# Moving DMA transposes, output stores and three pairs of state copies to other places and queues in a fused linear-attention and SwiGLU kernel

## The chip, the cores and the metric

The kernel runs on 1 core of one Trainium2 chip. The metric is device time in microseconds (us); profiled spans are about 2 us shorter than the timed runs of the same kernel. Engines: PE (TensorE), DVE (VectorE), ACT (ScalarE), POOL (GpSimd) and SP (SyncE, which here only issues DMAs). "Clock" is the share of its full clock that PE was granted.

## The reference, cut to what matters

Batches of 768 tokens go through causal linear attention with a decaying state; the result x goes through a SwiGLU layer.

```python
for b in range(nb):                       # blocks of the sequence, state carried along
    intra = einsum(qb, kb) * Dmask;  intra = einsum(intra, vb)
    inter = einsum(qb * lam_pow, kv_state)
    out[:, :, sl] = intra + inter
    kv_state = lam_block * kv_state + einsum(kb * rev_pow, vb)
# x: 3072 x 512
g = x @ w_gate;  silu = g / (1 + exp(-g))
return (silu * (x @ w_val)) @ w_out
```

Inputs and output are float32; the kernel multiplies in bfloat16. The reference's blocks have 64 tokens, the kernel's 128.

## The kernel before

The kernel works on 24 blocks of 128 tokens (4 batches of 6). A block needs three loads, issued on POOL (k and q are cast to bfloat16 on the way), then k and q transposed, `scores` (k times q), `cluster` (the output of attention and the new state), and its share of the feed-forward layer. Blocks 0 to 7 are transposed on PE, blocks 8 to 23 by DMA from the sync queue. The order of the program is the order of every engine and queue.

```python
    def load_kq(n):                                   # k and q of block n, cast to bf16
        t = ld.tile([128, 2, H, D], BF16, name="kq_nat", tag="kq")
        nc.gpsimd.dma_start(out=t[:, 0], in_=k5[b, j])
        nc.gpsimd.dma_start(out=t[:, 1], in_=q5[b, j])
    def load(n):
        load_kq(n)
        load_v(n, nc.gpsimd)                          # v stays float32
    # ... cut ...
    def transposes(n):
        t = apool.tile([128, 2, HP, BLK], BF16, name="qkT", tag="qkT", bufs=6)
        if n >= PE_T:                                 # PE_T = 8
            nc.sync.dma_start_transpose(out=t..., in_=state.pop(("kq", n))...)
        # ... else: on PE ...
    # ... cut: inside cluster(n, scores_of) ...
        if scores_of is not None:
            scores(scores_of)                         # needs transposes(scores_of)
        # ... x = xT on VectorE, matmuls "up", kv_st = kv_dec + up on VectorE ...
            bd = kv_bd[(n + 1) % 2]                   # the next block's inter matmuls need it
            for h2 in range(2):
                if n < PE_T:
                    nc.scalar.copy(out=bd[...], in_=st[r])
                else:
                    nc.gpsimd.tensor_copy(out=bd[...], in_=st[r])
    # ... cut: end of ffn_out ...
        nc.scalar.copy(out=osb, in_=op)
        nc.sync.dma_start(out=out[t0:t0 + 128, :], in_=osb)
    # ... cut: the schedule of the third tile of tokens ...
    for per in range(4):
        for pos in range(3):
            ffn_fc(2, 3 * per + pos)
            if pos == 2:
                ffn_out(*outs.pop(0))                 # one output store each
            if (per, pos) == (0, 2):
                scores(8)
                transposes(10)
            elif (per, pos) == (1, 0):
                cluster(8, 9)
                scale_v(10)
                load(12)
            elif (per, pos) == (1, 2):
                cluster(9, 10)
                transposes(11)
                scale_v(11)
                load(13)
            elif (per, pos) == (2, 1):
                cluster(10, 11)                       # needs transposes(11)
                # ... transposes(12), scale_v(12), load(14), and so on
```

## Time and profile before

| | before |
|---|---|
| median before the prediction (3 runs) | 247.18 us |
| profiled span, mean clock | 245.9 us, 0.976 |
| PE busy | 228.5 us, 93% |

The windows view gives the busy time of each engine in a stretch (number of instructions in brackets), then the clock, the share of the DMA engines and what they moved. Kernel before:

```profile
core 0: us, PE busy (x) PEld busy (x) DVE busy (x) ACT busy (x) POOL busy (x), PEclk, DMA share, GB/s
62.00:72.50 10.50, 10.28 (x111) 6.58 (x110) 5.10 (x9) 2.35 (x6) 3.35 (x6) 1.00 0.66 100
72.50:82.00 9.50, 2.54 (x32) 1.89 (x26) 2.50 (x5) 0.77 (x2) 6.78 (x9) 0.74 1.73 129
82.00:88.90 6.90, 6.68 (x46) 3.84 (x44) 2.57 (x4) 0.48 (x2) 4.06 (x6) 0.62 0.62 96
95.00:200.00 105.00, 104.37 (x722) 51.31 (x733) 47.50 (x69) 28.53 (x48) 44.21 (x62) 1.00 0.67 100
```

Nearly everywhere PE has no time to win: 104.37 of 105 us from 95 to 200. From 72.5 to 82 us it works 2.54 of 9.5 us. From 82 to 88.9 it is busy all the time, but with 46 instructions at a clock of 0.62: busy is not fast.

The chain that ended last, in order of time (start, length, what), around that hole:

```profile
62.31 2.32 PE yp L299 x10
69.05 2.54 PE yp L299 x11
...
72.76 9.01 DMA qkT<-kq_nat
81.78 0.05 issue
81.82 0.61 PE sp L207 x6
...
85.25 3.51 PE yp L299 x11
...
92.44 2.54 PE yp L299 x11
...
242.23 0.59 ACT osb L302
```

PE waits for a DMA transpose, and afterwards eleven matmuls that take 2.54 us elsewhere take 3.51. The timeline has PE's own waits, in brackets at the end of a line:

```profile
75.37 0.40 PE L221 MATMUL op<-qkT,kv_bd 128*128 128x128 bf16 x4 [0.91 <-POOL kv_bd L253]
81.82 0.61 PE L207 MATMUL sp<-qkT 64*128 64x128 bf16 x8 [6.05 <-DMA qkT<-kq_nat]
```

What stood on the sync queue (L303 is an output store, L184 a transpose):

```profile
65.28 0.36 SPq L303 DMA_DIRECT2D out_dram<-osb  x1
65.82 1.30 SPq L184 DMA_TRANSPOSE qkT<-kq_nat  x1
72.24 0.35 SPq L303 DMA_DIRECT2D out_dram<-osb  x1
72.76 9.09 SPq L184 DMA_TRANSPOSE qkT<-kq_nat  x2
```

The transpose at 72.76 us is that of block 11. The view of one line's instructions, for that transpose alone, gives its time to landing:

```profile
L184 SPq DMA_TRANSPOSE qkT<-kq_nat x1: 1488/1488/1488, 72.8 to 72.8; - x1
DMA to landing us min/median/max: 9.0/9.0/9.0
```

For the one at 65.82 us the same view says 3.1. So the transpose was issued late, behind a store, and then landed slowly.

### The profile page before, as it was taken

The page shows a single profiled execution, that of the slowest core. Times are in us where ns is not written, and L with a number is a line of the kernel's source. Part 1 is how long each engine was busy: PE and PEld are TensorE (multiplying, and loading weights), DVE is VectorE, ACT ScalarE, POOL GpSimd, SP SyncE. Part 2 cuts the span into 40 slices and gives each one's busy share as a digit, 9 for nine tenths or more (in the row PEclk, how much of TensorE's full clock was granted, in tenths as well). Part 3 has the DMA queues.
Part 4 walks back from the last instruction along what each step waited for, and adds up shares of the span by engine and source line. Part 5 has one row for each costly group of instructions (what it writes and reads, how often), then busy time and mean ns, then how long its engine had stood idle before and what let it go on. Part 6 is the DMA issues. An engine that isn't in the chain of part 4 may idle for free.

```text
span 245.9 us, 4376 instructions
## 1 busy us (share of the span) xinstructions
PE 228.5 (93%) x1730; PEld 125.0 (51%) x1754; DVE 104.8 (43%) x171; ACT 80.6 (33%) x158; POOL 114.9 (47%) x155
## 2 busy tenths in 40 slices
PE   7879999999991699999999999999999999999993
PEld 3456745788660464555455444455445444444441
DVE  1855636586552432562463354355256222322200
ACT  6556634646220023122212213313222222332121
POOL 8897979929078191447636750844331000000000
PEclk9999999999997599999999999999999999999998
DMA  6999999999929989998599595289301110111022
GB/s 131 195 190 211 188 218 163 188 207 147 162 33 155 136 107 172 108 128 117 99 146 119 94 204 126 52 120 131 87 0 45 43 41 2 45 43 43 19 109 85
DMA packets 83171, 28.32 MB, mean 115 GB/s; under 512 B 71056, under 2 KB 78736, under 8 KB 83152
## 3 DMA queue, kind: packets, MB, share of 16 engines
q0 software_dynamic: 57456, 16.26, 61.5%
q1 hardware_dynamic: 25696, 11.80, 21.8%
q8 instruction: 13, 0.21, 0.4%
q14 instruction: 6, 0.05, 0.1%
HBM read 28.32 MB, written 6.29 MB: 141 GB/s over the span
## 4 chain that ended last, share of the span: by engine, by line
PE 84%; ACT 6%; DMA 5%; DVE 2%; issue 2%; ACTq 0%
PE yp L299 26%; PE gp L273 25%; PE vp L273 24%; DMA qkT<-kq_nat 4%; PE op L227 4%; PE sp L207 3%; PE op L221 2%; ACT kv_bd L251 2%; DVE ssb L213 1%; ACT xT L232 1%; PE tp L193 1%; DMA lam_all<-in_lam_dram 1%; PE up L240 1%; ACT sil L288 1%; ACT L316 1%
## 5 line engine op out<-in xcount | busy, mean ns | idle before, releaser
L291 DVE TENSOR_TENSOR h_sb<-sil,vp 128x512 bf16<-128x512 bf16 (+3 forms) x90 | 51.7, 580 | 103.2 <-PE vp L273 90.0
L273 PE MATMUL gp<-xT,wg 128*128 128x512 bf16 (+3 forms) x361 | 77.3, 329 | 1.2 <-ACT xT L232 0.2
L273 PE MATMUL vp<-xT,wv 128*128 128x512 bf16 (+3 forms) x376 | 78.2, 331 | 0.1
L288 ACT ACTIVATE sil<-gp 128x512 bf16<-128x512 f32 (+3 forms) x90 | 45.6, 512 | 81.6 <-PE gp L273 78.4
L299 PE MATMUL yp<-wo,h_sb 128*128 128x512 bf16 x281 | 65.5, 383 | 0.5 <-issue 0.2
L273 PEld LDWEIGHTS <-wv 128*128 128x128 bf16 x376 | 35.5, 98 | 27.9 <-issue 0.2
L273 PEld LDWEIGHTS <-wg 128*128 128x128 bf16 x376 | 33.3, 98 | 26.5 <-issue 1.1
L299 PEld LDWEIGHTS <-h_sb 128*128 128x128 bf16 x288 | 28.5, 99 | 34.1 <-issue 1.6
L253 POOL CAST kv_bd<-kv_st 64x256 bf16<-64x256 f32 x26 | 10.3, 395 | 65.2 <-DVE kv_st L246 39.3
L213 DVE TENSOR_TENSOR ssb<-sp,mask 128x1024 bf16<-128x1024 f32 (+1 forms) x27 | 29.4, 1099 | 14.8 <-PE sp L207 14.7
L302 ACT COPY osb<-yp 128x512 f32<-128x512 f32 x24 | 14.1, 586 | 65.9 <-PE yp L299 65.9
L177 POOL TENSOR_TENSOR v_s<-v_raw,rev 128x512 bf16<-128x512 f32 x24 | 25.2, 1050 | 8.3 <-PE vp L273 4.9
L84 POOL DMA_DIRECT2D kq_nat<-in_k_dram x23 | 21.7, 943 | 0.1
L85 POOL DMA_DIRECT2D kq_nat<-in_q_dram x23 | 20.6, 895 | 0.7 <-DMA wv<-in_moe_w_val_dram 0.7
L79 POOL DMA_DIRECT2D v_raw<-in_v_dram x21 | 19.3, 919 | 0.0
L207 PE MATMUL sp<-qkT 64*128 64x128 bf16 x192 | 9.7, 222 | 8.3 <-DMA qkT<-kq_nat 6.1
L207 PEld LDWEIGHTS <-qkT 64*128 64x128 bf16 x192 | 5.7, 95 | 13.0 <-DMA qkT<-kq_nat 6.2
L227 PE MATMUL op<-ssb,v_s 128*64 128x128 bf16 x192 | 10.7, 229 | 0.6 <-DVE ssb L213 0.6
L234 DVE TENSOR_TENSOR xT<-op,qscale 128x512 bf16<-128x512 f32 x16 | 10.9, 680 | 0.0
L126 PE MATMUL warm_ps<-warm 128*128 128x512 bf16 x24 | 8.2, 479 | 1.3 <-DVE warm L121 1.2
L221 PE MATMUL op<-qkT,kv_bd 128*128 128x128 bf16 x80 | 7.8, 219 | 1.4 <-POOL kv_bd L253 0.9
L221 PEld LDWEIGHTS <-kv_bd 128*128 128x128 bf16 x80 | 5.9, 98 | 5.2 <-POOL kv_bd L253 1.2
(47 smaller groups left out, 91.2 us busy)
## 6 DMA issues: line engine op xcount, KB each, us to landing
out_dram<-osb SPq DMA_DIRECT2D x24, 256.0 KB, 2.1
v_raw<-in_v_dram POOLq DMA_DIRECT2D x21, 256.0 KB, 5.5
kq_nat<-in_k_dram POOLq DMA_DIRECT2D x23, 128.0 KB, 5.3
kq_nat<-in_q_dram POOLq DMA_DIRECT2D x23, 128.0 KB, 5.4
wg<-in_moe_w_gate_dram POOLq DMA_DIRECT2D x6, 256.0 KB, 5.8
wv<-in_moe_w_val_dram POOLq DMA_DIRECT2D x6, 256.0 KB, 6.3
wo<-in_moe_w_out_dram POOLq DMA_DIRECT2D x4, 384.0 KB, 8.0
v_raw<-in_v_dram SPq DMA_DIRECT2D x3, 256.0 KB, 5.5
```

What stands on the lines that cost most here:

```text
L79: eng.dma_start(out=v_raw[n], in_=v5[b, j])
L84: nc.gpsimd.dma_start(out=t[:, 0], in_=k5[b, j])
L85: nc.gpsimd.dma_start(out=t[:, 1], in_=q5[b, j])
L177: nc.gpsimd.tensor_tensor(out=t, in0=v_raw.pop(n), in1=bap(rev, [[1, H], [0, D]]), op=ALU.mult)
L207: nc.tensor.matmul(sp[:, h2, p, :], kT[n][r, p, :], qT[n][r, p, :], start=True, stop=True)
L213: nc.vector.tensor_tensor(out=s[:, :, ps], in0=sp[:, :, ps], in1=mask[:, :, ps], op=ALU.mult)
L221: nc.tensor.matmul(op[:, p, :], kv_bd[n % 2][:, p, :], qT[n][:, p, :], start=(p == 0), stop=False, skip_group_check=True)
L227: nc.tensor.matmul(op[64 * h2:64 * h2 + 64, p, :], v_s[n][:, 2 * p + h2, :], ssb[n][:, h2, p, :], start=(j == 0 and p == 0), stop=(p == HP ...
L273: nc.tensor.matmul(gv[tt, fc][i][:, lo:hi], w[c][:, mc, fs], xT[:, mc, t0 + lo:t0 + hi], start=(mc == 0), stop=(mc == MC - 1))
L288: nc.scalar.activation(sil[:, cs], gv[tt, fc][0][:, cs], AF.Silu)
L291: nc.vector.tensor_tensor(out=h_sb[tt][:, fc, cs], in0=sil[:, cs], in1=gv.pop((tt, fc))[1][:, cs], op=ALU.mult)
L299: nc.tensor.matmul(op, h_sb[tt][:, fc, sub * 128:(sub + 1) * 128], wo_sb[c][:, f, :], start=(fc == 0), stop=(fc == FC - 1))
```

## The change

Each DMA transpose follows its load in the program, so that only its own data holds it up; the sync queue keeps transposes alone, since stores go from the scalar queue; the state copies of blocks 8 to 11 (three pairs, as block 11 ends a batch and has none) go from POOL to ScalarE.

```diff
@@ load @@
         load_v(n, nc.gpsimd)
+        if n >= PE_T:
+            transposes(n)
@@ cluster @@
-                if n < PE_T:
+                if n < 12:
                     nc.scalar.copy(out=bd[r, :, 64 * h2:64 * h2 + 64], in_=st[r])
@@ ffn_out @@
-        nc.sync.dma_start(out=out[t0:t0 + 128, :], in_=osb)
+        nc.scalar.dma_start(out=out[t0:t0 + 128, :], in_=osb)
@@ schedule: the old places of the transposes go @@
                 scores(8)
-                transposes(10)
@@
                 cluster(9, 10)
-                transposes(11)
                 scale_v(11)
@@ ... likewise 8, 9, 12, 13, 14 (cut) ... @@
-                if pos == 0 and n + 3 < N:
-                    transposes(n + 3)
-                elif pos == 1 and n < N:
+                if pos == 1 and n < N:
```

More of the change, by code (lines that the diff above doesn't have):

```diff
@@ L388 @@
             transposes(7)
-            transposes(8)
             load(9)
@@ L395 @@
             cluster(7)
-            transposes(9)
             load(10)
@@ L423 @@
                 cluster(10, 11)
-                transposes(12)
                 scale_v(12)
@@ L428 @@
                 cluster(11, 12)
-                transposes(13)
                 scale_v(13)
                 load(15)
-                transposes(14)
     for tt in range(3, len(TILES)):
```

## The prediction

> **What bounds the kernel now.** TensorE. The busy table gives PE 228.5 of 245.9 us (93%); no other engine passes 47%. From 95 to 200 us the windows view shows PE busy 104.4 of 105 us at full clock. In the chain, PE stands still behind "DMA qkT<-kq_nat", which runs from 72.76 to 81.77 us: the transpose of block 11, which scores(11) waits for (PE idle 6.05 us, from 75.77 to 81.82). Afterwards PE runs at half clock until 88.8 us: four 256-column matmuls take 0.86 to 0.97 us in place of 0.44. The work from 81.82 to 88.76 (6.9 us) would take about 4.3 us warm, so the clock costs 2.6 us more. The Trainium skill ("TensorE: Matmul & The Clock Gate", "What's actually happening") says the clock falls to 4/8 after an idle window of about 3.4 us; the trace agrees (PEclk 0.74 and 0.80 from 72.5 to 95).
>
> Why that transpose was late: the sync queue is in order, and it stands behind the output store of 72.24 us. Its data had landed by about 65 us, and the DMA engines were idle from 69 to 72 us. Issued at 72.76, together with load(12) and load(13), it took 9.0 us to land; alone, transposes take 3.1 us (65.82) to 3.6 us (median).
>
> **What the change does.**
> 1. Transposes go right behind their loads, and the sync queue has no stores before them. Transpose 11 is issued near 65 us and lands near 70, before it is needed (75.8). Gain: 6.05 + 2.6 = 8.65 us, all on the critical path.
> 2. Transpose 12 comes next. PE now wants it at about 82.0 us, not 90.7. Load(12) starts near 70.6 (71.50 before); a transpose follows its k load by 5.7 us (103.85 to 109.52), so it issues near 76.3, beside load(13), and takes 5.2 us (as transpose 9 did beside load(10)): 81.5. Transpose 13 (issue near 82.5, 6 to 7 us beside load(14)) lands near 89, wanted at 89.9. Expected new waits: 0.7 us.
> 3. The three pairs of state copies (0.85 us a pair on POOL, 0.83 on ACT) sit before the silus of the next step in ACT's order. The 0.9 us wait of PE on kv_bd at 75.37 stays, since it hangs on kv_st, ready at 74.34. Silus move back by up to 2 us, inside the slack of four PSUM buffers: 0.3 us at most. POOL can issue load(14) near 80 us, not 86.6.
> 4. 24 stores go from ACT, 0.33 us each, off the critical path. The Trainium skill ("DMA: Bandwidth & Descriptors", "Issuing engines are not separate DMA queues") says only sequencer time is saved; no other effect expected.
> 5. From block 16 on, transposes already issued as their data landed: steady state and tail unchanged.
>
> **Prediction.** 247.2 - 8.65 + 0.7 + 0.3 = 239.5 us, 8 in 10 between 237.5 and 243. Chances: faster 0.88, within 2% 0.11, slower 0.01.
>
> **What would show it.** Right: transpose 11 issued before 68 us, landing within 5 us; no PE wait over 2 us for qkT after 70 us; PEclk 1.0 from 20 to 240 us; the 0.9 us kv_bd wait still there, now on ACT.
>
> **What would make it wrong.** Transpose 12 or 13 slowed to 9 us by loads: a new wait of 1 to 4 us on qkT, and over about 3.4 us the clock falls again, giving back half the gain. Or ACT's order holds the silus long enough for PE to wait for PSUM between 70 and 82 us.

## The result and the profile after

The changed kernel took 240.08 us (median of 4 runs, 239.86 to 240.26), against 247.61 us (4 runs) before. The ratio is 0.9697, 95% interval 0.9664 to 0.9731. Ratios here are the mean time of one kernel's fast runs over that of the other's of the same rounds, so not quite the ratio of the medians.

The same stretches after, in the windows view:

```profile
62.00:72.50 10.50, 9.92 (x89) 6.13 (x89) 4.94 (x8) 2.81 (x8) 3.23 (x4) 1.00 1.07 133
72.50:82.00 9.50, 8.83 (x102) 6.22 (x102) 5.38 (x9) 3.91 (x10) 7.84 (x10) 1.00 1.22 144
82.00:88.90 6.90, 6.85 (x54) 3.96 (x54) 3.04 (x6) 2.08 (x5) 4.88 (x6) 1.00 1.46 188
95.00:200.00 105.00, 104.37 (x703) 51.11 (x713) 45.55 (x66) 28.52 (x48) 42.77 (x59) 1.00 0.58 91
```

The hole is gone (8.83 us busy, not 2.54), and the clock stays full. The chain after, at the same four output groups of matmuls and the last copy of an output:

```profile
62.57 2.32 PE yp L301 x10
...
69.83 2.54 PE yp L301 x11
...
78.25 2.54 PE yp L301 x11
...
84.46 2.54 PE yp L301 x11
...
234.22 0.58 ACT osb L304
```

Set against the same lines before, each a milestone of the same work, this gives a ledger:

| up to | before | after | difference so far | added in this stretch |
|---|---|---|---|---|
| output 0 | 62.31 | 62.57 | +0.26 | +0.26 |
| output 1 | 69.05 | 69.83 | +0.78 | +0.52 |
| output 2 | 85.25 | 78.25 | -7.00 | -7.78 |
| output 3 | 92.44 | 84.46 | -7.98 | -0.98 |
| last copy on ACT | 242.23 | 234.22 | -8.01 | -0.03 |

The whole gain lies between outputs 1 and 3; after that both kernels run alike. Up to output 0 the change moves little; what the 0.26 us are was not looked into. The 0.52 us are a loss. The timeline after shows where:

```profile
69.18 0.60 PE L275 MATMUL vp<-xT,wv 128*128 128x256 bf16 x4 [0.36 <-DVE kv_st L248]
75.17 0.60 PE L275 MATMUL vp<-xT,wv 128*128 128x256 bf16 x4 [0.36 <-DVE kv_st L248]
76.02 0.40 PE L223 MATMUL op<-qkT,kv_bd 128*128 128x128 bf16 x4 [0.26 <-ACT kv_bd L253]
82.69 0.40 PE L209 MATMUL sp<-qkT 64*128 64x128 bf16 x8
```

With the copies on ACT, the silus stand behind them, and PE now waits twice for kv_st, which, as I read it, frees the PSUM buffer that PE needs next. At 75 us this replaces part of the old wait for kv_bd (0.36 + 0.26 in place of 0.91); at 69 us it is new. The last line is scores(12), without a wait. The landing view has why, first for transpose 11, then for 12:

```profile
L186 SPq DMA_TRANSPOSE qkT<-kq_nat x1: 2363/2363/2363, 65.0 to 65.0; - x1
DMA to landing us min/median/max: 4.8/4.8/4.8
L186 SPq DMA_TRANSPOSE qkT<-kq_nat x1: 1471/1471/1471, 77.3 to 77.3; - x1
DMA to landing us min/median/max: 5.0/5.0/5.0
```

Transpose 11 has landed by 69.8 us. Transpose 12 lands at 77.29 + 5.0 = 82.3 us, 0.4 us before PE wants it.

### The profile page after: what moved, and what is told of

Read it like the earlier page. It is cut to its first block, busy times and chain, and to the rows that moved or that the text cites. A ratio compares the mean times of both kernels' runs of the same rounds, so it can differ in the third digit from the quotient of the medians.

```text
span 237.9 us, 4361 instructions
## 1 busy us (share of the span) xinstructions
PE 226.4 (95%) x1730; PEld 123.7 (52%) x1754; DVE 104.5 (44%) x171; ACT 82.8 (35%) x164; POOL 112.4 (47%) x149
## 4 chain that ended last, share of the span: by engine, by line
PE 85%; ACT 6%; DVE 3%; issue 2%; DMA 1%; ACTq 0%
PE yp L301 26%; PE gp L275 25%; PE vp L275 24%; PE op L229 3%; PE sp L209 3%; ACT kv_bd L253 2%; PE op L223 2%; DVE ssb L215 2%; DMA lam_all<-in_lam_dram 1%; ACT xT L234 1%; PE tp L195 1%; PE up L242 1%; ACT sil L290 1%; ACT L318 1%; ACT L159 1%
## 5 line engine op out<-in xcount | busy, mean ns | idle before, releaser
L301 PE MATMUL yp<-wo,h_sb 128*128 128x512 bf16 x281 | 64.6, 379 | 0.4
L255 POOL CAST kv_bd<-kv_st 64x256 bf16<-64x256 f32 x20 | 7.9, 393 | 50.0 <-DVE kv_st L248 34.3
L253 ACT CAST kv_bd<-kv_st 64x256 bf16<-64x256 f32 x20 | 8.1, 403 | 8.7 <-DVE kv_st L248 7.5
L258 POOL TENSOR_TENSOR kv_dec<-kv_st,lamb 128x256 f32<-128x256 f32 x10 | 6.1, 608 | 9.7 <-DVE kv_st L248 9.1
```

Source lines behind the costliest of these rows:

```text
L301: nc.tensor.matmul(op, h_sb[tt][:, fc, sub * 128:(sub + 1) * 128], wo_sb[c][:, f, :], start=(fc == 0), stop=(fc == FC - 1))
```

## The experiments

Theory A: the gain is transpose 11 alone, which no longer stands behind the store of 72.2 us; a part of the loss before was the clock. Rivals: stores, early program places or copies each bring a share; or the slow landing has another cause. Twelve runs were made, of eleven kernels; all were correct. One execution of e3, slow (245.77 us), is left out of its ratio, but not of its median; the median of its three fast ones is 242.01 us.

| run | median us | ratio to before | 95% interval |
|---|---|---|---|
| the whole change again | 240.05 | 0.9715 | 0.9688 to 0.9742 |
| e1: transposes moved only | 239.93 | 0.9707 | 0.9681 to 0.9733 |
| e2: stores moved only | 240.50 | 0.9704 | 0.9675 to 0.9732 |
| e3: copies moved only | 242.88 | 0.9776 | 0.9727 to 0.9826 |
| e3 once more | 244.34 | 0.9868 | 0.9837 to 0.9900 |
| e4: whole change, copies back on POOL | 240.10 | 0.9714 | 0.9689 to 0.9739 |
| e5: before, dummy matmuls in the hole | 246.15 | 0.9929 | 0.9890 to 0.9969 |
| e6: before, loads 12 and 13 early | 242.72 | 0.9784 | 0.9745 to 0.9822 |
| e7: before, transpose 11 alone moved | 240.09 | 0.9702 | 0.9677 to 0.9726 |
| e8: e4, state update first on VectorE | 238.94 | 0.9669 | 0.9644 to 0.9693 |
| e9: before, v of 12 and 13 early | 244.00 | 0.9864 | 0.9845 to 0.9882 |
| e10: before, k and q of 12 and 13 early | 247.48 | 1.0018 | 0.9981 to 1.0056 |

### The whole change once more

No edit; the yardstick for e1, e4 and e8.

> The changed kernel again, unaltered, as the yardstick for the other runs of this chip. All theories: ratio to the kernel before 0.967 to 0.973, about 240 us.

It measured 240.05 us, ratio 0.9715: as expected.

### e1, e2 and e7: which part is needed?

e1 is the change with its stores and copies undone:

```diff
-        nc.scalar.dma_start(out=out[t0:t0 + 128, :], in_=osb)
+        nc.sync.dma_start(out=out[t0:t0 + 128, :], in_=osb)
-                if n < 12:
+                if n < PE_T:
```

> Only the transposes are moved; output stores stay on the sync queue, state copies of blocks 8 to 11 stay on POOL. Theory A (the whole gain is transpose 11 no longer waiting behind the store at 72.2 us): the full gain, 239.4 to 240.1 us, within 0.4 us of the whole change or slightly faster, since stores may now stand behind transposes but have three buffers of slack. Rival B (the stores must leave the sync queue as well, because they now wait behind transposes that wait for loads): part of the gain is lost, 241 us or more.

e2 is the kernel before with one line changed:

```diff
-        nc.sync.dma_start(out=out[t0:t0 + 128, :], in_=osb)
+        nc.scalar.dma_start(out=out[t0:t0 + 128, :], in_=osb)
```

> Only the output stores go to the scalar queue; transposes keep their places in the program, state copies stay on POOL. Theory A: on a sync queue that holds nothing but transposes, each one waits for its data alone, so transpose 11 issues near 65 us anyway: the full gain, 239.4 to 240.3 us. Rival B (the early place in the program is what counts): transpose 11 is still issued after 70 us and the time stays above 244 us.

e7 is the kernel before with one line moved:

```diff
                 transposes(10)
+                transposes(11)
@@
                 cluster(9, 10)
-                transposes(11)
```

> The kernel before with one line moved: transpose 11 goes right behind transpose 10, one store earlier in the sync queue's order. Theory A (the whole gain is this one transpose): transpose 11 is issued near 67 us, lands near 70 us, no stall, full gain: 239.5 to 240.5 us. Rival: transpose 12 or 13, still behind their stores, come too late now and take back 1 us or more.

All three give the full gain (0.9707, 0.9704, 0.9702; the whole change 0.9697 and 0.9715). Transpose 11, by the landing view of each, in the order e1, e2, e7:

```profile
L186 SPq DMA_TRANSPOSE qkT<-kq_nat x1: 1673/1673/1673, 65.0 to 65.0; - x1
DMA to landing us min/median/max: 3.5/3.5/3.5
L184 SPq DMA_TRANSPOSE qkT<-kq_nat x1: 1934/1934/1934, 63.5 to 63.5; - x1
DMA to landing us min/median/max: 4.0/4.0/4.0
L184 SPq DMA_TRANSPOSE qkT<-kq_nat x1: 1238/1238/1238, 67.3 to 67.3; - x1
DMA to landing us min/median/max: 3.2/3.2/3.2
```

Rival B falls in both its forms: neither leaving the sync queue to transposes nor early places for all of them is needed. Each of the two big parts alone lets this one transpose go by 68 us, and the second adds nothing. In e1 the stores now stand behind transposes (the sync queue's timeline has a store at 78.09, right after the transpose of 76.75), and PE has no new wait in its profile. e7's rival showed a trace of itself: a wait of 0.8 us for transpose 12 in the profiled run. e2's profile has two such waits, 1.0 us for transpose 12 and 0.5 us for transpose 13. Neither has an effect on the time that these intervals can resolve.

### e3 and e4: the state copies

e3 is the kernel before with `if n < PE_T` turned into `if n < 12` in front of the state copies. e4 is the whole change with that line back at `PE_T`.

> Only the state copies of blocks 8 to 11 go to ScalarE. Theory A: no gain, 247 to 248.5 us, transpose 11 still issued after the store near 72.5 us with PE waiting 5 us or more for it. Rival C (the copies matter on their own): 246 us or less.

> The whole change but with the state copies of blocks 8 to 11 back on POOL. Theory A: the copies on ScalarE cost about 0.3 us net (two waits of PE for a PSUM buffer behind kv_st, 0.36 us each, against a shorter wait for kv_bd), so this is 0.1 to 0.5 us faster than the whole change. Rival C (moving the copies helps, because POOL issues load 12 0.7 us earlier and load 14 4 us earlier, which transposes 12 and 13 need): transpose 12 comes too late and this is 0.5 to 2 us slower than the whole change.

e3 was a clear miss of theory A: the copies alone gained 2.2%, where nothing was expected. Transpose 11 still went late and behind a store, at 73.38 us, but landed in 5.2 us, not 9.0, and PE waited 2.3 us, not 6.05:

```profile
78.59 0.40 PE L207 MATMUL sp<-qkT 64*128 64x128 bf16 x8 [2.33 <-DMA qkT<-kq_nat]
```

The copies had been holding POOL, which issues the loads. Without them load 12 starts at 70.67 us, not 71.50, while the transpose goes 0.62 us later than before, so that it meets less of that load. That is an explanation after the fact; it led to e6, e9 and e10, but no run tests it for e3 itself.

The same kernel ran once more, to see whether this is luck:

> The run with only the copies moved once more, because it gained 5 us where none was expected and its times spread from 241.6 to 245.8 us. If the landing of transpose 11 depends on where it meets the v packets of load 12, it lands in anything from 4.5 to 9 us here, and the time goes with it: 241 to 247 us, with a spread above 2 us. If the copies remove a fixed cost, the landing is 5.2 us again and the times lie within 1 us of 242.5.

It took 244.34 us (243.74 to 245.99), with a landing of 5.7 us and a wait of 2.9 us. Neither guess held cleanly: the landing is in the lower part of the range both times, but the times of the two jobs spread over 4 us. The copies do help in both jobs; that they do so by the timing of a load, and not by a fixed cost, fits but is not shown.

e4 was no faster than the whole change: 0.9714 against 0.9715. PE lost the two waits for kv_st, but in the profiled run it waited 0.9 us for kv_bd on POOL again, and 0.9 us for transpose 12, which was issued at 77.72 us. So theory A's 0.1 to 0.5 us could not be found, and rival C's 0.5 to 2 us neither; within the resolution of about 0.3% the two homes of the copies are equal.

### e5: is the clock part of the loss?

```diff
         if scores_of is not None:
+            if scores_of == 11:
+                dummy = ps_f.tile([128, 512], FP32, name="dummy", tag="f")
+                for i in range(16):
+                    nc.tensor.matmul(dummy, warm[:, 0:128], warm, start=True, stop=True)
             scores(scores_of)
```

> The kernel before with 16 dummy matmuls of 512 columns (3.5 us warm) in the hole, after the state matmuls of block 10 and ahead of scores(11). They don't change when transpose 11 lands. Theory A (2.6 us of the loss are the clock, which falls because of the long idle stretch): the idle stretch shrinks to 2.5 us, the clock stays at full and the kernel gets 2 to 2.6 us faster, about 245 us. Rival D (matmuls after the hole are slow for another reason, such as the DMA traffic there): the matmuls at 82 to 89 us still take twice as long, and the time stays at 247 to 248 us.

The dummies add work and yet the kernel got faster, 246.15 against 248.12 us. Transpose 11 landed as before (8.9 us, so PE went on at 81.86 us). What changed is what came after, by the windows view:

```profile
76.00:79.50 3.50, 3.31 (x15) 1.34 (x14) 0.00 (x0) 0.00 (x0) 3.50 (x5) 1.00 1.52 145
79.50:81.86 2.36, 0.00 (x1) 0.01 (x2) 0.00 (x0) 0.00 (x0) 0.33 (x1) 1.00 2.86 101
81.86:88.00 6.14, 6.09 (x62) 4.31 (x64) 2.90 (x5) 1.62 (x4) 3.34 (x5) 1.00 0.90 116
```

62 instructions in 6.14 us at full clock, against 46 in 6.9 us at 0.62. Rival D falls; the clock is a loss of its own. The expected 2 to 2.6 us came out as 1.97 in the medians. Two of the four runs still had a clock of 0.990 and 0.993, and they were the slow ones (246.71 and 247.21 us, against 245.42 and 245.59 for the two at 1.0).

The clock records in the traces, looked at only afterwards, say more closely when the clock falls. In all 14 profiled runs every stretch of full or half clock, but the last, which the end cuts, lasts a whole multiple of 3.41 us. In the kernel before the clock is half from 76.97 to 87.21 us, three such units; in e3 and e9 for one, in e10 and in the second run of e3 for two. The windows view, set to these units (continued in steps of 3.41 us where the clock does not change), gives PE's busy time in the unit before the clock fell; for e5 and e6, where it did not fall, in the unit with the least work around the hole:

| run | unit, us | PE busy in it, us | clock in the next unit |
|---|---|---|---|
| e10 | 76.41 to 79.83 | 0.00 | half |
| e9 | 75.46 to 78.88 | 0.40 | half |
| e3 | 75.44 to 78.85 | 0.82 | half |
| e3 once more | 74.98 to 78.39 | 0.99 | half |
| before | 73.55 to 76.97 | 1.31 | half |
| e5 | 77.83 to 81.24 | 1.54 | full |
| e6 | 73.45 to 76.86 | 1.77 | full |

Counted over all 14 traces, with their ends, where PE runs out of work: half clock followed every unit at full clock with 1.34 us or less (19 of them), and none of more than 900 with 1.41 us or more. It came back after units with 3.20 us or more of PE work, and not after those with 2.42 us or less. So in these traces the share of a unit in which PE works decides, and not the length of one wait. Where the units begin differs from run to run, so the same wait can cost the clock in one run and not in another. This was worked out afterwards, with busy times of PE that are modelled; no run was made to test it.

### e6, e9 and e10: why did the transpose land in 9 us?

e6 is the kernel before with loads 12 and 13 moved up; e9 moves only the v halves of them, e10 only k and q, with three v loads put where load 12 was.

```diff
             load(11)
             scale_v(9)
+            load(12)                 # e9: load_v(12); e10: load_kq(12)
+            load(13)                 # e9: load_v(13); e10: load_kq(13)
@@
                 scale_v(10)
-                load(12)             # e9: load_kq(12); e10: load_v(12), (13), (14)
@@
                 scale_v(11)
-                load(13)             # e9: load_kq(13); e10: nothing; later load_kq(14) for load(14)
```

> The kernel before with loads 12 and 13 issued right behind load 11 (about 62 to 67 us); transpose 11 keeps its place behind the store of 72.2 us. Theory A (being late is nearly harmless; it is the collision with loads 12 and 13 that makes it land 9.0 us later): transpose 11 is issued near 72.8 us, lands in 3 to 4 us, PE waits under 1 us for it, and the time is 239 to 240.5 us. Rival E (transpose 11 is slow because of the store just ahead of it on its queue, or being late costs the same by itself): it still takes 7 us or more and the time is 245 us or more.

In e6 transpose 11, still behind its store at 72.90 us, landed in 3.5 us. Being late and standing behind a store therefore does not by itself make it slow; in that form rival E falls. But the gain was only 2.2%, against the 239 to 240.5 us expected: the collision had moved on to transpose 10, issued at the same time as before (65.95 us), which now met loads 12 and 13 and took 9.1 us. The landing view of e6, transposes 10 and 11:

```profile
L184 SPq DMA_TRANSPOSE qkT<-kq_nat x1: 1489/1489/1489, 66.0 to 66.0; - x1
DMA to landing us min/median/max: 9.1/9.1/9.1
L184 SPq DMA_TRANSPOSE qkT<-kq_nat x1: 1295/1295/1295, 72.9 to 72.9; - x1
DMA to landing us min/median/max: 3.5/3.5/3.5
```

I had not checked what the earlier loads would meet. The miss is stronger evidence than the hit: the same two transposes swapped their landing times when the loads moved.

> The kernel before with only the v halves of loads 12 and 13 issued early (behind load 11); their k and q loads stay, so transpose 11 still meets k and q packets of 128 B, but no v packets of 4 KB. Theory F (the slow landing of 9 us comes from meeting the v packets; k and q packets alone slow it mildly): transpose 11 is issued near 72.8 us and lands in 4 to 5.5 us, the wait of PE shrinks from 6 us to 1 to 2.5 us, and the time is 240.5 to 243 us. Rival G (any load makes it slow): it lands in 8 to 9 us, time 246 us or more.

> The mirror of it: the k and q loads of 12 and 13 are issued early, and three v loads (12, 13, 14) are issued where load 12 was, 71.5 to 74.2 us, so transpose 11 meets v packets alone. Theory F: transpose 11 lands in 7 us or more and the v packets take several times the 160 ns that they take alone; PE waits 4 us or more; 244 to 248 us. Rival G (it is the number of packets in front that counts, and these are few): it lands in 3 to 5 us and the time is near 240 us.

Transpose 11 in e9 (meets k and q packets alone), then in e10 (meets v packets alone), by the landing view:

```profile
L184 SPq DMA_TRANSPOSE qkT<-kq_nat x1: 1511/1511/1511, 73.1 to 73.1; - x1
DMA to landing us min/median/max: 5.9/5.9/5.9
L184 SPq DMA_TRANSPOSE qkT<-kq_nat x1: 1496/1496/1496, 72.7 to 72.7; - x1
DMA to landing us min/median/max: 8.7/8.7/8.7
```

e10 came out as theory F said (landing 8.7 us, wait 5.7 us, 247.48 us). e9 went the right way but less far than I wrote: 5.9 us, not 4 to 5.5; a wait of 3.0 us, not 1 to 2.5; 244.0 us, not 240.5 to 243. So beside k and q packets the landing took 2.8 us more than the 3.1 us alone, and where v packets took part as well (before) or alone (e10), 8.7 to 9.0 us. Packets counted in the trace agree (mean duration of the 4 KB v packets that ended in each stretch, and number of transpose packets):

```
kernel before   79.0 to 79.5 us:  10 v packets, 689 ns;  120 transpose packets
kernel before   82.0 to 82.5 us:   5 v packets, 161 ns;    0 transpose packets
e10             79.5 to 80.0 us:  12 v packets, 1016 ns;  73 transpose packets
kernel before  129.0 to 129.5 us:  0 v packets;          411 transpose packets
```

Where the two meet, both crawl. Why they do is not shown by any run; e10 also has three v loads in a row, and transposes 11 and 12 in flight together, so its share is not exactly that of one load: 190 v packets ended while its transpose 11 was landing, against 64 in the kernel before. Nor is meeting v packets enough to be slow: in e3, too, 64 of them ended during the landing, and it took 5.2 us. There the v packets were through at 77.13 us, 1.0 us after the transpose's own first packet (76.16); in the kernel before the two overlapped from 76.39 to 80.80 us. How long they overlap goes with the slowness, but which of the two holds up the other is open.

The store ahead of the transpose has a part that the text above leaves out. In the kernel before and in e9 the transpose's own packets start only when those of that store are about through: 1.2 us after the issue for transpose 10 of the kernel before (no load in flight), but 2.7 us for its transpose 11 and 2.8 us for that of e9. From the first to the last of its own packets the three took 1.4, 5.3 and 2.6 us. So about 1.5 us of the slow landing lies before the transpose has moved anything. Transpose 12 of the changed kernel, with loads in flight and no store ahead, started 1.7 us after its issue, so the store may account for about 1 us of this (an estimate); no run tests that for transpose 11.

### e8: a version that beats both

e4's profile leaves a wait of 0.9 us for kv_bd, which hangs on kv_st, which stands behind the scaling of xT on VectorE. e8 is e4 with the two swapped, for blocks 8 on:

```diff
-        else:
+        elif j == NB - 1:
             nc.vector.tensor_tensor(out=x, in0=op, in1=qscale, op=ALU.mult)
@@ after kv_st
+            if n >= PE_T:
+                nc.vector.tensor_tensor(out=x, in0=op, in1=qscale, op=ALU.mult)
```

> As the run with the copies back on POOL, and on VectorE the state update kv_st goes ahead of the scaling of xT (blocks 8 on). kv_st then comes 0.68 us sooner, and the wait of PE for kv_bd at about 75 us (0.9 us) should shrink to 0.2 to 0.3 us. Theory A: 0.4 to 0.8 us faster than that run, 0.6 to 1.2 us faster than the whole change. Rival: the wait moves elsewhere (transpose 12 is just in time, so PE waits for it instead), and the two are equal within 0.2 us.

It took 238.94 us (238.85 to 239.29); no run of it overlaps one of the whole change of the same job (239.70 to 240.83). It is 1.1 us faster than the change, as expected, and 1.2 us faster than e4, more than expected. The waits view (us in all, times, longest) has the wait at 0.3 us, as foreseen:

```profile
PE op L223 <- POOL kv_bd L257: 0.3, 1, 0.3
```

In its profiled run there was no wait for transpose 12 either (issued at 76.17 us), which may be the rest.

## Why the prediction was right

The prediction was 239.5 us, range 237.5 to 243; 240.08 us was measured.

- **The bound and the hole: right.** The stretch between outputs 1 and 3 gave 7.78 + 0.98 = 8.76 us in the profiled runs, where 6.05 + 2.6 = 8.65 had been written. e7 shows that one transpose is all of it, e5 that the clock is a part of its own. The profile taken as the base had a clock of 0.976, though; most other runs of the kernel before had 0.986 and were shorter (in the job of e1 seven spans at 0.986 have a mean of 244.9 us, three at 0.976 one of 245.8). So 8.65 is a little more than the mean loss, which fits the measured 7.4 and 7.5 us in place of the forecast 7.7. The text has half clock until 88.8 us; the clock record has it from 76.97 to 87.21.
- **Transpose 12 just in time: right.** Forecast: issued 76.3, landing in 5.2 us at 81.5, wanted at 82.0. Measured: 77.29, 5.0 us, 82.3, 82.7. Transpose 13: forecast landing near 89, wanted 89.9; measured 82.84 + 6.7 = 89.5, wanted 90.4. The 0.7 us of new waits were 0 in the profiled run; e2 (1.5 us in two waits), e4 (0.9 us) and e7 (0.8 us) show that it could have gone the other way. That the sum came out within 0.6 us is therefore partly luck: these 0.7 us did not occur, and the hole was read from a profile that is longer than most runs of its kernel. The two errors have opposite signs.
- **The copies: size right, place wrong.** 0.3 us was allowed at most. The ledger has 0.52 us lost before output 1, part of it won back before output 2. The text said that the wait of 0.9 us for kv_bd stays and moves to ACT; it fell to 0.26 us, and two waits of 0.36 us for kv_st came in. What the text missed is that the copies held up the loads, and that moving them alone gains 1.3 to 2.2% in the old order (e3).
- **The stores: right for this kernel, but incompletely reasoned.** "No other effect" holds once the transposes have moved: e1, with its stores on the sync queue, equals the whole change. Alone, though, moving the stores is worth the full gain (e2), because the transposes no longer stand behind them. The prediction did not see that parts 1 and 2 of the change are each sufficient.
- **Cause of the 9.0 us: half told.** "Together with load(12) and load(13)" was right (e6), but the text does not say which packets: with v in flight the landing was slower than with k and q alone (e9, e10), though not in e3, and part of the time is the store ahead.
- **The Trainium skill.** "DMA: Bandwidth & Descriptors", section "Issuing engines are not separate DMA queues", says DMAs of all issuing engines run on the same 16 engines and interleave. No run here tests the bandwidth. The prediction took from that section that a second queue saves sequencer time only, and expected no other effect; in e2 it changed what an issue waits for, 9.2 us for one transpose (72.76 to 63.52), and with it the whole gain.

## What to carry to other kernels

In an in-order DMA queue, look at what each issue stands behind: a transfer whose data is ready can wait for a store whose data is not. One moved line can be worth a whole restructuring, so test the parts alone before crediting all of them. When a hole closes, ask at once which transfer is needed next, and what it will meet in flight. To judge whether a wait will cost the clock as well, add up PE's work around it and not only the length of the wait.

## What the Trainium skill lacked or had wrong

- "DMA: Bandwidth & Descriptors", section "Rules for kernel authors", says that a transpose next to ordinary DMAs needs nothing. For correctness the runs agree (all results were correct). For time it lacks a warning: the same 256 KB transpose landed in 3.1 us alone, in 5.9 us beside k and q loads (e9), in 9.0 and 9.1 us beside loads with their v part (before, e6; but 5.2 us in e3), and in 8.7 us beside v loads (e10), and 4 KB packets of such a load went from about 160 ns to 689 and 1016 ns.
- "DMA: Bandwidth & Descriptors", section "Issuing engines are not separate DMA queues", lacks that moving a DMA to another engine's queue also changes which waits it stands behind: e2, with one line changed, has a ratio of 0.9704.
- "TensorE: Matmul & The Clock Gate", section "HAM oscillation — how this bites in real kernels", gives the rule of no PE-idle gaps over about 3.4 us. In these runs the length of the gap does not decide: in e3 the clock fell with a wait of 2.3 us (0.54 from 78.6 to 82.3 us), in e6 it stayed at 1.00 through one of 3.1 us, and in the kernel before it fell 1.2 us after PE had gone idle (75.77 to 76.97 us). The busy time in a unit of 3.41 us does: half clock followed 0.00 to 1.34 us, never 1.41 us or more (table and count under e5). A gap under the rule's figure is not safe.
- "TensorE: Matmul & The Clock Gate", section "What's actually happening", says that the phase of the window varies the warm-up at the start from run to run. It lacks that a stall in mid-kernel varies too: waits of 6.05 us (before) and 5.7 us (e10) cost 10.24 and 6.83 us of half clock, and the kernel before had clocks from 0.976 to 0.986 in one job, with spans of 244.2 to 246.0 us. It also gives no busy time below which the clock falls; here it lies between 1.34 and 1.41 us of 3.41.
